# Attention and feed-forward on one core: from an order spread over loops and rates to one order made by a list scheduler in the kernel, with the first tiles transposed by TensorE

## The chip, the cores and the metric

The kernel runs on one NeuronCore of a Trainium2 chip. The time is device microseconds of one execution, from three runs; the trace is of one profiled execution. TensorE (PE) multiplies and takes a weight load before each matmul; VectorE (DVE), ScalarE (ACT) and GpSimd (POOL) do the element-wise work; SyncE (SP) issues the DMAs. Each engine works through its own instructions in the order in which they were written for it.

## The reference

Four batches, eight heads, 768 positions, head size 64. Attention is banded: a position sees the `n_global` = 8 first positions and the `n_local` = 96 positions up to itself, with a bias of a slope per head times the distance. The output, as 3,072 tokens of 512 values, goes through a layer norm and a feed-forward net of 512 to 2,048 to 512 with a residual.

```python
def _attn_ref(q, k, v, n_global, n_local):
    scores = scale * np.matmul(q, k.transpose(0, 1, 3, 2))
    keep = is_global | is_local
    scores = np.where(keep, scores + bias[None], -1e9)
    a = np.exp(scores - np.max(scores, axis=-1, keepdims=True))
    a = a / (np.sum(a, axis=-1, keepdims=True) + 1e-09)
    return np.matmul(a, v)

def _moe_ref(x, g_ln, w_ch1, w_ch2):
    xn = (x - mu) / np.sqrt(var + 1e-06) * g_ln
    return x + np.maximum(xn @ w_ch1, 0.0) @ w_ch2
```

The two weight matrices arrive as 64-bit floats, 16.8 MB together.

## The kernel before

A **tile** is 128 positions of one batch, all heads; there are 24, in the order of `TILES`: first tile 0 of batches 3, 2, 1, 0 (t = 0 to 3, the *first tiles*, which see one block of keys), then tiles 1 to 5 of each batch (t = 4 to 23), which see two blocks. A **chunk** c is two tiles, 256 tokens.

Every operand of a matmul is split into two fp16 parts, high and low, and three products of the four (four in the scores) are added up in PSUM.

**Attention of a tile** (`attention`): load k, q, v (256 KB each, L108); split them (ACT makes the high part, DVE or POOL the low one: L177/L178, L199/L200, L186/L187); transpose k and q by DMA (`kT`, `qT`, L180, L202) and copy q's halves by two DMAs (L208); then by groups of heads, two groups in a first tile and four in another: score matmuls (L234), mask and row minimum on DVE (L239), exponential on ACT (L243), split into `pn` (high part on ACT for t < 4, else on DVE, L246/L248; low part on POOL, L249), transpose by DMA (`pT`, L251), product with v (L259 to L261). Then the quotient (L265), and in `norm` the mean and variance (L272, L273), the power on POOL (L276), the scaling (L279 to L281) and a last DMA transpose into `xT` (L282).

**Feed-forward.** `ffn1` multiplies `xT` by w1 and puts a 512-column bank into two fp16 parts (L335 on ACT, L336 on DVE); `ffn2` multiplies by w2 (L344) and adds the residual (L348); L350 stores. For t < 4 `ffn1` goes tile by tile with 128 columns (the groups called `f` at L330 to L332), after that by chunk with 256 columns (`f_None`).

**Weights** (`weight`): 16 pieces of 1 MB, each loaded (L115) and put together by ACT, DVE, ACT, DVE, ACT, DVE (L151 to L157), in three buffers.

**What sets the order.** The loops write the work as generators. `run(main, side, rate)` takes `rate` steps of the side work for each step of the main work (0.6, 2.0, 2.0, 0.5 at the start, `RATE` = 1.6 after), one tile ahead (`AHEAD`); a dictionary `ORDER` ties single instructions to others. From that the framework's own scheduler (`schedule_with_timeline_sim=True`) makes the order of each engine. At the start this is

```python
    run(f1w(), tokens(1), 0.6)      # w1 pieces and ffn1 of tile 0, beside tile 1
    run(f1(1), tokens(2), 2.0)
    run(f1(2), tokens(3), 2.0)
    run(f2w(), f1(3), 0.5)          # w2 pieces, beside ffn1 of tile 3
    run(seq(ffn2(0, 1), ffn2(2), ffn2(3)), side(3 * CT + AHEAD), RATE)
    for c in range(2, NC):          # ffn(c): ffn1 of the chunk, ffn2 of its two tiles
        g = side((c + 2) * CT + AHEAD)
        run(ffn(c), extremes(g) if c == 3 else g, RATE)
```

All DMAs are issued from SP, in one queue.

Of the kernel before, what the change touches and what calls it, by code (L numbers as in the profile page):

```python
# [12 lines left out]
I32 = mybir.dt.int32  # L13
# [60 lines left out]

@with_exitstack
def banded(ctx, tc, q, k, v, n_global, n_local, g_ln, w1, w2, out, flag):
    nc = tc.nc
    vec, act, pool, sp, pe = nc.vector, nc.scalar, nc.gpsimd, nc.sync, nc.tensor
    load = sp
# [11 lines left out]
    def chain(prev, ins):  # L91
        if prev is not None:
            tc.add_manual_dep(ins.ins, prev.ins.name, NOSYNC, reason="groups of one bank in turn")
        return ins

    marks = {}

    def mk(key, ins):

        marks[key] = ins  # L100
        if ORDER.get(key) in marks:
            tc.add_manual_dep(ins.ins, marks[ORDER[key]].ins.name, NOSYNC, reason="order")

    place = {bi: t for t, bi in enumerate(TILES)}

    def fetch(src, name, b, i):
        f = p2.tile([P, H, D], F32, tag="ld", name=f"{name}f{b}_{i}", bufs=6)
        mk(f"L{place[b, i]}", load.dma_start(out=f, in_=src[b, :, i * P:(i + 1) * P, :].rearrange("h p d -> p h d")))  # L108
        return f

    early = {name: fetch(src, name, *TILES[0]) for name, src in (("k", k), ("q", q))}

    def piece(src, name):
        st = p3.tile([P, 2, 512], I64, tag="st", name="st" + name, bufs=3)
        mk("D" + name, load.dma_start(out=st, in_=src))  # L115
        return st

    def piece1(j, c):
        return piece(w1[2 * c * P:2 * (c + 1) * P, j * 512:(j + 1) * 512].rearrange("(a p) n -> p a n", a=2), f"1_{j}_{c}")

    early["w"] = piece1(0, 0)
    cnt = counts(tc, const, load, n_global, n_local)
    ng, nl = cnt[:, 0:1], cnt[:, 1:2]
# [15 lines left out]
    big = const.tile([P, NF], F32, name="big")  # L139
    less = const.tile([P, 1], F32, name="less")  # L140
    pool.memset(less, -0.5001)
    wm = const.tile([P, 16], F32, name="wm")

    def weight(st, dh, dl, name, n):

        words = st.rearrange("p a n -> p (a n)").bitcast(I32).rearrange("p (n two) -> p n two", two=2)
        lo, hi = words[:, :, 0], words[:, :, 1]  # L150
        mk("A" + name, act.activation(out=lo, in_=st.rearrange("p a n -> p (a n)").bitcast(U32).rearrange("p (n two) -> p n two", two=2)[:, :, 0], func=AF.Relu, scale=2.0 ** -29, bias=less))  # L151
        vec.scalar_tensor_tensor(out=lo, in0=hi, scalar=SIGN, in1=lo, op0=ALU.bitwise_and, op1=ALU.bitwise_or)
        act.activation(out=hi.bitcast(F32), in_=hi.bitcast(F32), func=AF.Abs, scale=2.0 ** -111, accum_out=big[:, n:n + 1])
        vec.scalar_tensor_tensor(out=hi, in0=hi, scalar=3, in1=lo, op0=ALU.logical_shift_left, op1=ALU.bitwise_or)
        u = st.bitcast(F32).rearrange("p a (n two) -> p a n two", two=2)[:, :, :, 1]
        act.activation(out=dh, in_=u, func=AF.Copy)
        vec.tensor_tensor(out=dl, in0=u, in1=dh, op=ALU.subtract)  # L157

    def weights1(j, c):
        sl, cs = slice(j * 512, (j + 1) * 512), slice(2 * c, 2 * c + 2)  # L160
        weight(piece1(j, c) if j or c else early["w"], w1h[:, cs, sl], w1l[:, cs, sl], f"1_{j}_{c}", 2 * j + c)

    def weights2(f):
        fs = slice(2 * f, 2 * f + 2)
        weight(piece(w2[2 * f * P:2 * (f + 1) * P, :].rearrange("(a p) n -> p a n", a=2), f"2_{f}"), w2h[:, fs, :], w2l[:, fs, :], f"2_{f}", NF // 2 + f)


    mv = const.tile([P, B * NT, 2], F32, name="mv")
    blocks = {}
# [12 lines left out]

    def values(b, i):
        vf = fetch(v, "v", b, i)
        vn = p2.tile([P, H, P], F16, tag="vn" if i else "vn0", name=f"vn{b}_{i}", bufs=3 if i else 2)
        act.activation(out=vn[:, :, :D], in_=vf, func=AF.Copy, scale=VS)  # L186
        vec.scalar_tensor_tensor(out=vn[:, :, D:], in0=vf, scalar=VS, in1=vn[:, :, :D], op0=ALU.mult, op1=ALU.subtract)  # L187
        return vn

    def attention(t, x, xT, at):  # L190
        b, i = TILES[t]
        if i == 1 and b:
            blocks[b, 0] = keys(b, 0), values(b, 0)
            yield
        kT = keys(b, i)
        qf = early["q"] if t == 0 else fetch(q, "q", b, i)
        yield
        qn = p2.tile([P, H, P], F16, tag="ld", name=f"qn{t}", bufs=6)
        act.activation(out=qn[:, :, :D], in_=qf, func=AF.Copy, scale=-QS)  # L199
        vec.scalar_tensor_tensor(out=qn[:, :, D:], in0=qf, scalar=-QS, in1=qn[:, :, :D], op0=ALU.mult, op1=ALU.subtract)  # L200
        qT = p2.tile([P, 2 * H, P], F16, name="qT")
        mk(f"q{t}", sp.dma_start_transpose(out=qT[:, :H, :], in_=qn.rearrange("p h d -> p (h d)")))  # L202
        yield
        for here, there in ((slice(0, D), slice(D, P)), (slice(D, P), slice(0, D))):
            if t == 0:
                vec.tensor_copy(out=qT[here, H:, :], in_=qT[there, :H, :])
            else:
                load.dma_start(out=qT[here, H:, :], in_=qT[there, :H, :])  # L208
# [12 lines left out]
        nm = p2.tile([P, H], F32, name="nm")
        mn = p2.tile([P, H], F32, name="mn")
        sm = p2.tile([P, H], F32, name="sm")
        r = p2.tile([P, H], F32, name="r")
        for g in range(H // gh):
            yield
            T = p2.tile([P, gh, W], F32, tag="T", name=f"T{t}_{g}", bufs=3)
            ps = ps_s.tile([P, gh, W], F32, tag="s", name=f"s{t}_{g}")
            last = None
            for u in range(gh):  # L230
                h = g * gh + u
                for n_ in range(nb):
# [441 lines left out]
```

## Time and profile before

| | |
|---|---|
| time, median of 3 runs | 698.7 us (697.59 to 702.15) |
| span of the profiled execution | 697.8 us |
| PE, DVE, ACT, POOL busy | 596.8, 392.7, 291.9, 157.5 us |
| mean granted clock of TensorE | 0.971 of full speed |
| DMA moved | 93.30 MB, 134 GB/s over the span |

The span runs from the first to the last instruction; the profiled execution's own time is not given beside it. Of the three runs the median is 0.9 us above the span. A busy PE is not PE at its peak: matmuls overlap, and the busy time is the union of their durations. "Idle before" is the time an engine stood still before an instruction, with what released it. A row's `f_None<-xT,w1h` means that a matmul writes `f_None` from `xT` and `w1h`.

### The profile page before, as it was taken

To read this page: it belongs to the slowest core of one execution; us is meant where nothing else is said; L and a number is where in the kernel's file an instruction comes from. 1 tells how busy PE (TensorE), PEld (TensorE's weight loads), DVE (VectorE), ACT (ScalarE), POOL (GpSimd) and SP (SyncE) were. 2 spreads that over 40 slices of the span, in tenths; PEclk is the share of its full clock that TensorE was granted. 3 is DMA by queue.
4 is the path that set the end of the run, shared out by engine and by line. 5 is a ranking of instruction groups with operands and counts; after the bars stand their busy time and mean duration, and the time that the engine had idled before them with its cause. 6 is when DMAs were issued, how large, how long until landed. Compare 5 with 4: busy or idle time off the path is not lost. (4 is left out here: it accounts for less than half of the span.)

```text
span 697.8 us, 14209 instructions
## 1 busy us (share of the span) xinstructions
PE 596.8 (86%) x5602; PEld 426.6 (61%) x5602; DVE 392.7 (56%) x976; ACT 291.9 (42%) x752; POOL 157.5 (23%) x141
## 2 busy tenths in 40 slices
PE   0107698998499988999999999899989999999995
PEld 0106576775377576587496586496576586694762
DVE  4887978725567777565456456365445456342111
ACT  4886959323424442354254254253243254140110
POOL 0111304213213313332221331222231232120000
PEclk9999799999599999999999999999999999999999
DMA  9999999936888766676948746856853855231001
GB/s 230 221 278 262 237 260 187 172 58 115 163 161 143 129 139 136 134 148 117 178 90 151 140 96 134 150 106 123 159 118 73 151 82 94 69 62 31 16 1 36
DMA packets 264731, 93.30 MB, mean 134 GB/s; under 512 B 254416, under 2 KB 254416, under 8 KB 264656
## 3 DMA queue, kind: packets, MB, share of 16 engines
q1 hardware_dynamic: 264656, 92.31, 65.2%
q8 instruction: 46, 0.75, 0.5%
q14 instruction: 29, 0.24, 0.1%
HBM read 37.23 MB, written 6.29 MB: 62 GB/s over the span
## 5 line engine op out<-in xcount | busy, mean ns | idle before, releaser
L344 PE MATMUL f<-w2h,h_None 128*128 128x512 f16 x640 | 197.0, 380 | 0.0
L330 PE MATMUL f_None<-xT,w1h 128*128 128x256 f16 x640 | 176.1, 275 | 2.9 <-DVE h_None L336 2.4
L331 PE MATMUL f_None<-xT,w1h 128*128 128x256 f16 x640 | 176.1, 275 | 0.0
L332 PE MATMUL f_None<-xT,w1l 128*128 128x256 f16 x640 | 175.9, 275 | 0.0
L249 POOL TENSOR_TENSOR pn<-T,pn 128x512 f16<-128x512 f32 x88 | 109.2, 1243 | 218.2 <-DVE pn L248 111.6
L344 PEld LDWEIGHTS <-h_None 128*128 128x128 f16 x960 | 91.9, 98 | 99.7 <-issue 1.6
L344 PE MATMUL f<-w2l,h_None 128*128 128x512 f16 x320 | 121.8, 381 | 0.0
L331 PEld LDWEIGHTS <-w1h 128*128 128x128 f16 x896 | 90.7, 101 | 28.6 <-issue 19.0
L330 PEld LDWEIGHTS <-w1h 128*128 128x128 f16 x896 | 90.8, 101 | 16.5 <-DMA xT<-xn 6.9
L332 PEld LDWEIGHTS <-w1l 128*128 128x128 f16 x896 | 90.8, 101 | 7.6
L243 ACT ACTIVATE T<-T,mn 128x256 f32<-128x256 f32 (+1 forms) x192 | 92.4, 484 | 3.6
L335 ACT ACTIVATE h_None<-f_None 128x512 f16<-128x512 f32 x80 | 47.2, 592 | 107.1 <-PE f_None L332 107.0
L336 DVE SCALAR_TENSOR_TENSOR h_None<-f_None,h_None 128x512 f16<-128x512 f32 x80 | 54.7, 684 | 50.8 <-ACT h_None L335 50.8
L239 DVE CUSTOM_DVE_ANT_0 T<-s,mask 128x256 f32<-128x256 f32 (+1 forms) x192 | 67.1, 396 | 25.5 <-PE s L234 25.0
L234 PE MATMUL s<-kT,qT 128*128 128x128 f16 x704 | 55.2, 226 | 25.5 <-DMA qT<-qn 14.2
L259 PE MATMUL pv<-vn,pT 128*128 128x64 f16 x352 | 40.9, 196 | 39.9 <-DMA pT<-pn 39.8
L234 PEld LDWEIGHTS <-qT 128*128 128x128 f16 x704 | 47.4, 101 | 34.6 <-DMA qT<-qn 14.3
L330 PE MATMUL f<-xT,w1h 128*128 128x128 f16 x256 | 50.4, 237 | 17.1 <-DMA xT<-xn 17.1
L248 DVE CAST pn<-T 128x512 f16<-128x512 f32 x80 | 39.9, 502 | 42.8 <-ACT T L243 39.0
L259 PEld LDWEIGHTS <-pT 128*128 128x128 f16 x352 | 32.4, 99 | 50.1 <-DMA pT<-pn 47.9
L178 POOL TENSOR_TENSOR kn<-kf,kn 128x512 f16<-128x512 f32 x20 | 25.5, 1273 | 121.0 <-ACT kn L177 121.0
L276 POOL TENSOR_TENSOR rs<-rs,half 128x1 f32<-128x1 f32 x24 | 22.4, 931 | 133.5 <-DVE rs L275 133.5
(96 smaller groups left out, 804.0 us busy)
## 6 DMA issues: line engine op xcount, KB each, us to landing
st<-in_moe_w_ch_dram SPq DMA_DIRECT2D x16, 1024.0 KB, 7.4
vf<-in_v_dram SPq DMA_DIRECT2D x27, 256.0 KB, 3.6
kf<-in_k_dram SPq DMA_DIRECT2D x26, 256.0 KB, 3.8
qf<-in_q_dram SPq DMA_DIRECT2D x24, 256.0 KB, 3.3
out_dram<-x SPq DMA_DIRECT2D x24, 256.0 KB, 2.4
qT<-qT SPq DMA_DIRECT2D x46, 128.0 KB, 2.4
pT<-pn SPq DMA_TRANSPOSE x88, 3.3
kT<-kn SPq DMA_TRANSPOSE x27, 4.1
```

Source lines behind the costliest of these rows:

```text
L234: last = chain(last, pe.matmul(ps[:, u, n_ * P:(n_ + 1) * P], lhsT=qT[:, a * H + h, :], rhs=use[n_][0][:, h, :], start=(a == 0), stop=(a = ...
L239: vec.tensor_tensor_reduce(out=T[:, u, :], in0=ps[:, u], in1=mask, scale=1.0 / Z, scalar=3e38, op0=ALU.add, op1=ALU.min, accum_out=nm[:, h ...
L243: mk(f"e{t}_{g}", act.activation(out=T[:, u, :], in_=T[:, u, :], func=AF.Exp, scale=-1.0, bias=mn[:, h:h + 1], accum_out=sm[:, h:h + 1]))
L248: vec.tensor_copy(out=pn[:, :, 0, :], in_=T)
L249: pool.tensor_tensor(out=pn[:, :, 1, :], in0=T, in1=pn[:, :, 0, :], op=ALU.subtract)
L259: last = chain(last, pe.matmul(pv[:, h, :], lhsT=ph, rhs=vv[:, h, :D], start=(n_ == 0), stop=False))
L330: last = chain(last, pe.matmul(ps[:, a], lhsT=w1h[:, kk, fs], rhs=xT[:, kk, cols], start=(kk == 0), stop=False))
L331: last = chain(last, pe.matmul(ps[:, a], lhsT=w1h[:, kk, fs], rhs=xT[:, NK + kk, cols], start=False, stop=False))
L332: last = chain(last, pe.matmul(ps[:, a], lhsT=w1l[:, kk, fs], rhs=xT[:, kk, cols], start=False, stop=(kk == NK - 1)))
L335: mk("h" + key, act.activation(out=hh[:, 0], in_=ps, func=AF.Relu))
L336: mk("l" + key, vec.scalar_tensor_tensor(out=hh[:, 1], in0=ps, scalar=0.0, in1=hh[:, 0], op0=ALU.max, op1=ALU.subtract))
L344: pe.matmul(ps, lhsT=hh[:, a, :], rhs=w, start=(f == 0 and n_ == 0), stop=(f == NF - 1 and n_ == 2))
```

## The change

Nothing is written in order any more. Each piece of work becomes an `Op` with its engine, an estimated duration, what it reads and writes, and a function that writes its instructions; a DMA also has an estimated transfer. `Plan.order` adds the edges that reused buffers bring, computes for each op the time that is still needed from its start to the end of the main chain (all ffn1 and ffn2 pieces, stretched by 1.13, plus 6 us for what feeds them), and then runs a list scheduler over PE, ACT, DVE, POOL and SP: on each engine, of the ops whose inputs are there, the one with the greatest need. Matmuls that read what a DMA brings are offered only 2 us after the estimated landing if something else is there. The ops are then written in that order inside `tc.manual_schedule()`, so that each engine keeps it.

```diff
-AHEAD = 1
-RATE = 1.6
+FEW = 2 * CT
-ORDER = {"D1_0_1": "q0", "L1": "q0", "L2": "p0_1", "L3": "p1_1"}
-ORDER.update({f"X{n}": f"l{2 + n // 8}_{2 * n % 16}" for n in range(16)})
+class Plan:
+    SEEN = {"DMA": 1.6, "PE": 0.25}
+    MARGIN = {"DMA": 2.0}
+    def order(self, chain, stretch, lead):
...
+        for o in reversed(line):
+            most = left.get(o, 0.0)
+            for p in o.behind:
+                extra = lead if p in rank and o not in rank else 0.0
+                most = max(most, need[p] + o.took + self.seen(o) + extra)
+            need[o] = max(most, o.took)
...
+        def offer(o):
+            t = max([o.after] + [end[p] for p in o.before])
+            m = max([t] + [end[p] + self.MARGIN["DMA"] for p in o.before if p.xfer is not None]) if o.engine == "PE" else t
+            known[o.engine].append((t, m, -need[o], place[o], o))
...
+                at = max(free[e], min(c[0] for c in known[e]))
+                now = [c for c in known[e] if c[1] <= at] or [c for c in known[e] if c[0] <= at]
+                c = min(now, key=lambda c: (c[2], c[3]))
...
+            free[e] = at + o.took
+            if o.xfer is not None:
+                dma = max(dma, free[e]) + o.xfer
+                end[o] = dma + self.SEEN["DMA"]
...
+    def split(ps, hi, lo, scale, r, w):
+        op("ACT", 0.64, lambda: act.activation(out=hi(), in_=ps(), func=AF.Copy, scale=scale), r=r, w=[(w, "hi")])
+        op("DVE", 0.72, low, r=[*r, (w, "hi")], w=[(w, "lo")])
+
+    def flip(src, r, name):
+        ps = psum(ps_2, "f2", [P, 4, P], name)
+        def emit():
+            for j in range(4):
+                pe.transpose(ps()[:, j, :], src()[:, j * P:(j + 1) * P], eye())
+        op("PE", 0.9, emit, r=[r, eye], w=[ps])
+        return ps
...
+    def first(ts):
...
+                f = raw[name, t]
+                ps = flip(lambda f=f: f().rearrange("p h d -> p (h d)"), f, f"{name}t{t}")
+                o = buf(p2, "kT0" if name == "k" else "qT", 2, [P, 2, 4, P], F16, f"{name}0_{t}")
+                split(ps, lambda o=o: o()[:, 0], lambda o=o: o()[:, 1], scale, [ps], o)
...
+                    for j in range(4):
+                        for n_, (a, c) in enumerate(((0, 0), (0, 1), (1, 0), (1, 1))):
+                            pe.matmul(ps()[:, j, :], lhsT=qT[side, a, j, :], rhs=kT[side, c, j, :], start=(n_ == 0), stop=(n_ == 3))
...
+                ps = flip(lambda T=T: T().rearrange("p j w -> p (j w)"), T, f"pt{t}_{e}")
+                pT = buf(p2, "pT", 4, [P, 2, 4, P], F16, f"pT{t}_{e}")
+                split(ps, lambda pT=pT: pT()[:, 0], lambda pT=pT: pT()[:, 1], 1.0, [ps], pT)
...
+                vec.tensor_scalar(out=xf(), in0=x().rearrange("p h d -> p (h d)"), scalar1=mv[:, t, 0:1], scalar2=rs(), op0=ALU.subtract, op1=ALU.mult)
+                vec.tensor_mul(out=xf(), in0=xf(), in1=gb)
...
+            ps = flip(xf, xf, f"xt{t}")
...
+    def ffn1(c, f):
+        n = CT * P
...
+    first(range(CT))
+    for j in range(NK):
+        for c_ in range(NK // 2):
+            weights1(j, c_)
+    first(range(CT, FEW))
+    for f in range(NF // 2):
+        weights2(f)
+    for c in range(2):
+        for f in range(0, NF, 2):
+            ffn1(c, f)
+    ffn2(0, 1)
+    ffn2(2, 3)
+    for t in range(FEW, B * NT):
+        attention(t)
+    for c in range(2, NC):
+        for f in range(0, NF, 2):
+            ffn1(c, f)
+        for n_ in range(CT):
+            ffn2(c * CT + n_)
...
+    line = plan.order(main, 1.13, LEAD)
+    with tc.manual_schedule():
+        for o in line:
+            o.emit()
+LEAD = 6.0
```

In the first tiles k, q, the exponentials and the normed x stay 32-bit floats, PE transposes them four 128 x 128 blocks at a time into a bank of `ps_2` (which ffn2 uses too), and ACT and DVE split them out of PSUM. Two heads lie in one block, so a score matmul there contracts 64 rows, and there are four products of the parts instead of a stacked pair. `ffn1` of tiles 0 to 3 is by chunk. Tile 4 loads and transposes k of batch 0's first tile again. `pT` has 4 buffers instead of 3; `mask0` and the identity `eye` lie in buffers of `h`. The low part of k of a reloaded first tile goes from DVE to POOL. The two counts are loaded from ACT's queue. The sixteen `extreme` reductions may not start before 250 + 10 n us of the plan.

## Rows read from the trace of the kernel before

**Rows 1.** The page: busy time of each engine with its share of the span and its instructions, and the span in 40 slices, PE's busy tenths.

```profile
span 697.8 us, 14209 instructions
...
PE 596.8 (86%) x5602; PEld 426.6 (61%) x5602; DVE 392.7 (56%) x976; ACT 291.9 (42%) x752; POOL 157.5 (23%) x141
...
PE   0107698998499988999999999899989999999995
```

**Rows 2.** The timeline of PE (start us, us, engine, line, operation, out<-in, shapes, count) in two dense stretches, and between them pieces of the chain that ended last (start us, us, what, count).

```profile
654.76 0.27 PE L330 MATMUL f_None<-xT,w1h 128*128 128x256 f16 x1
...
656.72 0.27 PE L330 MATMUL f_None<-xT,w1h 128*128 128x256 f16 x1
...
480.21 0.45 PE s L234 x8
...
627.77 20.72 PE f L344 x96
...
160.00 0.19 PE L259 MATMUL pv<-vn,pT 128*128 128x64 f16 x1
...
160.32 0.19 PE L261 MATMUL pv<-vn,pT 128*128 128x64 f16 x1
```

**Rows 3.** Instructions by tile or line: duration in ns (min/median/max), first and last start in us. The first two are ffn1 by chunk (t from 4 on) and by tile (t < 4), then the residual add.

```profile
L330 PE MATMUL f_None<-xT,w1h x640: 269/273/418, 189.4 to 673.5; 128*128 128x256 f16 x160
L330 PE MATMUL f<-xT,w1h x256: 216/219/314, 55.4 to 146.0; 128*128 128x128 f16 x128
...
L348 DVE SCALAR_TENSOR_TENSOR x<-f,x x24: 654/690/692, 135.7 to 690.2; 128x512 f32<-128x512 f32 x24
```

**Rows 4.** Windows: stretch in us, its length, busy us (instructions) of PE, PE's weight loads, DVE, ACT and POOL, granted clock, DMA's share, GB/s.

```profile
0.00:40.00 40.00, 5.76 (x56) 4.47 (x57) 26.18 (x67) 26.57 (x53) 4.33 (x11) 1.00 0.92 240
40.00:80.00 40.00, 18.16 (x238) 16.74 (x238) 35.85 (x73) 33.29 (x73) 5.73 (x4) 0.96 1.03 258
80.00:120.00 40.00, 34.60 (x389) 27.12 (x389) 33.09 (x53) 31.07 (x58) 12.49 (x8) 0.87 1.06 223
120.00:160.00 40.00, 39.23 (x459) 28.09 (x457) 21.67 (x48) 13.75 (x36) 10.08 (x8) 1.00 0.72 124
160.00:189.40 29.40, 17.55 (x184) 11.69 (x183) 18.25 (x56) 11.68 (x40) 7.76 (x7) 0.77 0.70 131
189.40:690.20 500.80, 481.35 (x4282) 338.51 (x4281) 256.56 (x678) 175.59 (x494) 117.10 (x104) 0.99 0.58 111
```

**Rows 5.** What PE waited for up to 189 us: us in total, times, longest us.

```profile
PE pv L259 <- DMA pT<-pn: 22.9, 9, 11.8
PE f L330 <- DMA xT<-xn: 17.1, 4, 15.5
PE s L234 <- DMA qT<-qn: 14.2, 2, 13.8
PE f L344 <- ACT w2h L156: 6.4, 2, 4.0
```

**Rows 6.** Groups of instructions by form over the whole span, costliest first: line, engine, operation, out<-in, shapes, count | busy us, mean ns of one | idle before us and what ended it. L152, L154 and L157 are the DVE steps of a weight piece, L336 and L335 split a bank of 512 columns out of PSUM.

```profile
L234 PE MATMUL s<-kT,qT 128*128 128x128 f16 x704 | 55.2, 226 | 25.5 <-DMA qT<-qn 14.2 <-DMA qT<-qT 4.1 <-DVE nm L239 4.1
L336 DVE SCALAR_TENSOR_TENSOR h_None<-f_None,h_None 128x512 f16<-128x512 f32 x80 | 54.7, 684 | 50.8 <-ACT h_None L335 50.8
...
L335 ACT ACTIVATE h_None<-f_None 128x512 f16<-128x512 f32 x80 | 47.2, 592 | 107.1 <-PE f_None L332 107.0
...
L152 DVE SCALAR_TENSOR_TENSOR st<-st 128x1024 int32<-128x1024 int32 x16 | 21.2, 1324 | 6.3 <-ACT st L151 6.2
L279 DVE SCALAR_TENSOR_TENSOR xs<-x,mv,gb 128x512 f32<-128x512 f32 x24 | 20.4, 849 | 0.0
...
L154 DVE SCALAR_TENSOR_TENSOR st<-st 128x1024 int32<-128x1024 int32 x16 | 19.6, 1222 | 1.6 <-ACT st L153 1.6
...
L157 DVE TENSOR_TENSOR w2l<-st,w2h 128x1024 f16<-128x1024 f32 x8 | 10.7, 1332 | 0.6 <-ACT w2h L156 0.6
L157 DVE TENSOR_TENSOR w1l<-st,w1h 128x1024 f16<-128x1024 f32 x8 | 9.7, 1213 | 2.4 <-ACT w1h L156 2.4
...
L178 DVE TENSOR_TENSOR kn<-kf,kn 128x512 f16<-128x512 f32 x7 | 4.8, 688 | 7.5 <-ACT kn L177 7.5
...
L206 DVE COPY qT<-qT 64x1024 f16<-64x1024 f16 x2 | 0.8, 422 | 0.0
```

**Rows 7.** One more window, and DVE's first instruction in the timeline.

```profile
40.00:60.00 20.00, 4.59 (x45) 4.59 (x45) 19.61 (x38) 17.91 (x38) 4.73 (x3) 1.00 0.97 249
...
4.81 0.69 DVE L178 TENSOR_TENSOR kn<-kf,kn 128x512 f16<-128x512 f32 x1 [4.81 <-ACT kn L177]
```

**Rows 8.** DMA: SP's issue of the transposes of pT and of the copies of qT (duration in ns, min/median/max, first and last start), and what the queue moved from 0 to 100 us (packets, MB, share of 16 engines).

```profile
L251 SPq DMA_TRANSPOSE pT<-pn x88: 1231/1264/2406, 26.5 to 623.0; - x88
...
L208 SPq DMA_DIRECT2D qT<-qT x46: 462/580/1467, 30.9 to 577.8; - x46
...
q1 hardware_dynamic: 39660, 24.34, 99.0%
```

**Rows 9.** What PE waited for from 189.4 us on, and the landing of pT after 200 us.

```profile
PE pv L259 <- DMA pT<-pn: 16.8, 19, 2.5
PE f_None L330 <- DVE h_None L336: 2.4, 2, 2.1
...
DMA to landing us min/median/max: 3.0/3.2/5.1
```

More of the change, by code (lines that the diff above doesn't have):

```diff
@@ L75, in banded @@
+LOOK = 0.5
+EAGER = 3.0
 @with_exitstack
@@ L89, in banded @@
     ps_2 = ctx.enter_context(tc.tile_pool(name="ps_2", bufs=2, space=PSUM))
[L91 to L108, printed above, removed]
-        return f
@@ L111, in banded @@
[L111 to L122, printed above, removed]
+    plan = Plan()
@@ new lines, in columns, with fetch, half_of @@
+    def columns(n, each):
+        return n * (each / 2400.0 + 0.0025)
+    def fetch(src, name, b, i, engine="SP"):
+        f = buf(p2, "ld", 6, [P, H, D], F32, f"{name}f{b}_{i}")
+        eng = act if engine == "ACT" else sp
+        dma(lambda: eng.dma_start(out=f(), in_=src[b, :, i * P:(i + 1) * P, :].rearrange("h p d -> p h d")), 1.6, w=[f], took=0.8, engine=engine)
+        return f
+    def half_of(t):
+        b, i = TILES[t]
+        return b, i
+    raw = {}
+    for name, src in (("k", k), ("q", q)):
+        raw[name, 0] = fetch(src, name, *TILES[0])
@@ L138, in banded @@
     w2l = const.tile([P, NF, DM], F16, name="w2l")
[L139 to L157, printed above, removed]
+    op("POOL", 0.8, lambda: make_identity(nc, eye()), w=[eye])
@@ L183, in values @@
[L183 to L187, printed above, removed]
-        return vn
-    def attention(t, x, xT, at):
+        weight(w2[2 * f * P:2 * (f + 1) * P, :].rearrange("(a p) n -> p a n", a=2), w2h[:, fs, :], w2l[:, fs, :], f"2_{f}", NF // 2 + f)
@@ L191, in attention, with join @@
+    def join(parts, whole):
+        plan.wrote[whole] = [o for p in parts for o in plan.wrote[p]]
+    xs, xTs, hs = {}, {}, {}
+    def attention(t):
         b, i = TILES[t]
-        if i == 1 and b:
-            blocks[b, 0] = keys(b, 0), values(b, 0)
-            yield
         kT = keys(b, i)
[L196 to L208, printed above, removed]
@@ L287, in tokens @@
+        op("DVE", 0.77, lambda: vec.scalar_tensor_tensor(out=xn()[:, 1, :], in0=xf(), scalar=rs(), in1=xn()[:, 0, :], op0=ALU.mult, op1=ALU.subtract), r=[xf, rs, (xn, "hi")], w=[(xn, "lo")])
         c, at = divmod(t, CT)
         if at == 0:
-            xTs[c] = p3.tile([P, 2 * NK, CT * P], F16, tag="xT", name=f"xT{c}", bufs=2)
-        xs[t] = xpool.tile([P, H, D], F32, tag="x", name=f"x{t}")
-        yield from attention(t, xs[t], xTs[c], at)
-    gs = const.tile([P, NK], F32, name="gs")
-    load.dma_start(out=gs, in_=g_ln.rearrange("(c p) -> p c", p=P))
@@ new lines, in banded @@
+    op("POOL", 0.1, lambda: pool.memset(ones, 1.0), w=["ones"], after=300.0)
+    op("DVE", 0.9, ranges, r=["cnt", *(("big", n_) for n_ in range(NF))], w=["ok"], after=450.0)
+    op("DVE", 1.0, products, r=["gs"], w=["wm", "wx"], after=460.0)
+    op("DVE", 0.7, limits, r=["wx"], w=["ok", "sums"], after=470.0)
+    op("DVE", 0.5, verdict, r=[("mv", t) for t in range(B * NT)], w=["ok", "sums"])
+    pf = psum(ps_1, "f1", [1, 3], "pf")
+    op("PE", 0.1, lambda: pe.matmul(pf(), lhsT=ones, rhs=sums, start=True, stop=True), r=["ones", "sums"], w=[pf])
```

657 lines of the change are left out of this document (417 added, 240 removed).

## The prediction

> **What bounds the kernel now.** I read the page first: PE is busy for 596.8 of 697.8 us, but the slices show that the first five and the eleventh are far from full [rows 1]. Busy time is a poor measure of pipelined matmuls, so I took the pitch, the distance from one start to the next, out of dense stretches [rows 2]: eighteen matmuls of 256 columns in 1.96 us are 0.109 us each; 96 of 512 columns in 20.72 us are 0.216; eight of 128 columns in 0.45 us are 0.056; eleven steps of 64 columns in 0.32 us are 0.029. The work by pitch: a chunk's ffn1 is 16 x 12 matmuls of 256 columns, 20.9 us; its ffn2 is 96 of 512 columns, 20.7; a tile that sees two blocks has 32 score matmuls and 48 products, 1.8 + 1.4 = 3.2 us.
>
> Then the marks in time [rows 3]: chunk 2's ffn1 begins at 189.4, the last residual add at 690.2. What PE still has to do from the first of these is ten chunks (416.4) and the attention of 18 tiles (57.3), **474 us**, in 500.8: only **27 us** are lost there. Ahead of it PE has ffn1 of four tiles in 128 columns (768 x 0.056 = 43), ffn2 of four tiles (41.5), attention of four first tiles (64 scores, 96 products: 6.4) and of two others (6.4): 97 us in 189.4, so **92 us are lost** before chunk 2. The windows [rows 4] say beside what: DVE is busy for 26.2 + 35.9 + 33.1 + 21.7 + 18.3 = 135.0 of 189.4 us (0.71) and ACT for 116.4, DMA is full to 120 us, PE is not. The waits name the releasers [rows 5]: until 189 us PE waits for transposing DMAs (pT 22.9 us, xT 17.1, qT 14.2), little for weights. So the first part is set by chains through DMA, ACT and DVE in which no engine is full, and behind it by DVE's sheer work; the second part is set by PE.
>
> **DVE's work before chunk 2.** It doesn't get less. Of it, 16 weight pieces cost 21.2 + 19.6 + 10.7 + 9.7 = 61.2 us [rows 6]. The split of pT out of PSUM is new for DVE (before, POOL made that low part): 8 x 0.684 by the row of a 512-column split out of PSUM = 5.5 us. The normed x of a first tile takes two instructions for one: four more, of nothing to 0.85 (the scaling with a scalar and a vector) each; I take 0.69, kn's subtraction, which it is nearest to by operands and size, so 2.8. Two copies for tile 0's qT go (0.8). The splits of k, q and x are the same count, from PSUM instead of SBUF (0.684 against 0.688: nothing). Sum 142.5 us. ACT's eight high parts of pn become eight of pT (0.59 each), so it stays at 116: not the bound.
>
> DVE starts at 4.8 us. With what fill? Before, 0.71 on the whole, 0.90 from 40 to 80 us, 0.98 at best [rows 4, 7]. With a scheduler that always has two chains (weights and tiles) to choose from, and shorter chains, I take the row of 0.90: chunk 2 at 4.8 + 142.5/0.90 = **163 us**; at 0.98 it is 150, at 0.71 it is 205. PE's own path allows it: ffn1 of chunk 0 now waits for tile 1 as well and begins when DVE has done two first tiles, masks and two pieces (about 32 us of work, so near 40 us, against 55.4); chunk 1 needs all four tiles and w1's eight pieces, about 77 us of DVE work or 90 us; behind it 20.9 + 41.5 + 6.4 us make 159.
>
> **What goes and what comes elsewhere.** Twenty DMA transposes (kT, qT, two pT and xT of four tiles) and six copies of qT leave SP's queue, 20 x 1.26 + 6 x 0.58 = 28.7 us of issuing [rows 8], and 5.2 + 0.8 MB (256 and 128 KB each) leave DMA; nearly all of it ran in the first 100 us, where 24.3 MB at 99% are on the queue [rows 8]. So the loads of weights and of tiles 4 and 5 come sooner; without it DVE would stay short of input. One load of k with its split and transpose comes in for tile 4, on SP behind the loads of that tile; POOL, busy for 10 of 80 us at the start [rows 4], gets its low part and loses eight of pn. Two small loads move from SP's to ACT's queue, ahead of ACT's first split, on which DVE waits until 4.8 us [rows 7]: two issues, at worst 1.2 us by the copies' row.
>
> PE gets 80 transposes of 32-bit blocks, which the trace doesn't show. Nearest is a 128-column matmul: 0.056 us at the pitch, 0.226 by itself [rows 2, 6], so 4.5 to 18 us; I take 18, since they come four at a time and are waited for. Sixty-four more score matmuls (contracting 64 rows) are 3.6 us, ffn1 of four tiles in 256 columns is 384 x 0.109 = 41.9 for 43. All of it lies ahead of chunk 2, where PE has 92 us to spare and would keep 163 - 118 = 45: nothing on the sum. Below nothing they don't go, as no PE work is taken out. Were that cover gone (PE bound from 40 us on), they would cost their 18 us.
>
> [...]
>
> **The steady part.** It has the same PE work, 474 us. Of the 27 us lost, 16.8 are waits for pT in 19 of the products, 2.4 for h, and the rest is mostly the clock (0.99 over 500.8 us) [rows 4, 9]. A pT lands 3.0 to 5.1 us after its issue [rows 9]; the new order puts the product at least 1.3 + 1.6 + 1.6 us behind its issue by the plan, and 2 us more if other work is there. So most of these waits should go: I take **10 us** (4 to 25). The sixteen `extreme` reductions and the tail's small DVE work lie in DVE's idle half (256.6 busy of 500.8 us); if it were full there, PE would wait for h.
>
> **Sum.** 163 + 474 + 10 + 7.6 from the start of the last residual add to the span's end (690.2 to 697.8, unchanged: the last add and store) + 0.9 by which the median stands above the span = **655 us**.
>
> **The rivals.**
> *Better fill.* DVE at 0.98 and 4 us lost: 150 + 474 + 4 + 8.5 = 636. For it: DVE did it for 20 us. Against: only there.
> *Half the fill.* In-order ACT and DVE hand each piece to and fro six times, three weight buffers allow no more than three pieces under way, and a fixed order can't take what happens to be ready: fill 0.80, chunk 2 at 183, 15 lost, 680. The same time would come of the clock: if the transposes leave it at half while ffn1 of both first chunks runs, its 41.9 us take 83.8, and PE's path is 40 + 83.8 + 41.5 + 6.4 + 10 for the transposes and scores of tiles 2 and 3, 182 us. Against it: 0.96 with a PE less than half busy [rows 4]. [...]
> *No gain at the start.* Fill stays 0.71, chunk 2 at 205: 698, no change. For it: the fill was low with a scheduler before too. Against: DMA, then full, is relieved of a fifth.
> *Slower.* The order is fixed from estimates, and PE meets each of the 80 later products (20 tiles x 4) before its pT has landed, with everything queued behind it on PE. Before it was 16.8/80 = 0.2 us each. From 0.75 us each, 60 us in place of my 10, the kernel is over 1% slower; at 0.9 it is 718. It decides only if DVE, ACT or SP run behind the plan all the time; they have idle halves, which speaks against it.
> *The order isn't kept*, and the framework sorts anew: then only the first tiles' shorter chains remain. I put them at a third of the 54 us that PE waited for qT, pT and xT [rows 5], 18 us: 680.
>
> **How the numbers follow.** Chances: forecast 0.55 (643 to 670), better fill 0.15, half the fill or the clock 0.13, no gain 0.07, slower 0.07, order not kept 0.03. The likeliest is 655. Leaving out some 0.1 on either side gives 636 to 687. One per cent, 7 us, is about what a measurement can tell here; faster by more than that are the forecast, better and half fill and the order not kept: 0.86; within it 0.07; slower 0.07.
>
> **What would show it.** First matmul of ffn1 near 40 us; chunk 2's (the first ffn1 that follows an xT made by DMA) near 163; DVE's busy share before it near 0.9; DMA below full in the first 100 us; waits of PE for pT after it under 5 us; transposes of 0.06 to 0.23 us. I'd be wrong if chunk 2 starts on time but the 474 us stretch by more than 25, or if DVE's share stays at 0.7.

## The result, and the profile after

The changed kernel takes **653.96 us** (median of 4 runs, 653.24 to 655.26) against 698.14 us of the kernel before beside it (695.75 to 702.15): ratio 0.9364, 95% interval 0.9326 to 0.9403. Forecast were 655.0 us and a range of 636 to 687.

First the page of after (busy us, share, instructions; PE's busy tenths in 40 slices; the DMA queue's packets, MB, share), to lay beside [rows 1].

```profile
span 653.5 us, 13626 instructions
...
PE 607.1 (93%) x5362; PEld 432.5 (66%) x5362; DVE 407.3 (62%) x983; ACT 290.8 (45%) x753; POOL 148.9 (23%) x139
...
PE   6478669979999999999999999999999999999995
...
q1 hardware_dynamic: 245904, 87.06, 64.6%
```

The hole that was at the eleventh slice is gone, and so are the eights that follow it. What is left lies in the first nine slices.

The marks, which answer to [rows 3]: ffn1 by line (ns min/median/max, first and last start in us), the PE timeline where chunk 2 begins (start us, us, line, out<-in), and the residual add.

```profile
L635 PE MATMUL f<-xT,w1h x768: 272/273/421, 38.8 to 624.3; 128*128 128x256 f16 x192
...
172.99 0.61 PE L590 MATMUL s<-kT,qT 128*128 128x128 f16 x8
173.44 0.27 PE L635 MATMUL f<-xT,w1h 128*128 128x256 f16 x1
...
L667 DVE SCALAR_TENSOR_TENSOR x<-f,x x24: 671/688/693, 145.9 to 645.6; 128x512 f32<-128x512 f32 x24
```

The first ffn1 is at 38.8 us (before 55.4). A chunk has 64 of L635's matmuls, so the 129th is chunk 2's first: 173.4 us (before 189.4). From there to the last ffn2's end are 472.1 us, and 8.0 more to the span's end: 173.4 + 472.1 + 8.0 = 653.5.

Windows, as [rows 4] (stretch, length, busy us of PE, weight loads, DVE, ACT, POOL, granted clock, DMA share, GB/s):

```profile
0.00:40.00 40.00, 21.46 (x157) 17.09 (x158) 27.81 (x85) 27.77 (x70) 3.39 (x12) 1.00 0.75 191
40.00:80.00 40.00, 30.54 (x249) 24.16 (x249) 34.45 (x70) 33.86 (x75) 2.93 (x2) 0.87 0.75 218
80.00:120.00 40.00, 34.29 (x328) 29.39 (x327) 34.58 (x57) 28.62 (x53) 3.77 (x4) 0.91 0.56 147
120.00:150.00 30.00, 25.15 (x174) 12.56 (x173) 28.80 (x49) 19.62 (x43) 10.01 (x8) 0.91 0.86 183
150.00:173.40 23.40, 23.40 (x177) 12.42 (x176) 12.51 (x31) 5.62 (x18) 5.03 (x5) 0.97 0.78 168
173.40:645.90 472.50, 472.25 (x4286) 336.89 (x4283) 268.37 (x691) 175.34 (x498) 123.77 (x109) 1.00 0.63 118
```

PE is full from 150 us on, before chunk 2 begins, and stays so to the end. All but some 0.7 us of what is lost is lost ahead of 150. What PE waited for in the whole span (us, times, longest), against [rows 5, 9]:

```profile
PE xt L401 <- DVE xs L527: 13.1, 3, 7.4
PE f L635 <- DVE h L643: 6.5, 1, 6.5
PE kt L401 <- DMA kf<-in_k_dram: 4.8, 2, 4.7
PE f L658 <- DVE x L667: 3.9, 1, 3.9
PE pt L401 <- DVE pT L388: 3.3, 1, 3.3
```

No wait for a pT that DMA brings is left (before 22.9 us up to 189 and 16.8 behind it). The pT of after land 3.1/3.4/5.5 us (min/median/max) after their issue from 174 us on, no sooner than before; the products come later. With issues and first products paired in their order, a product starts 6.5/11.7/22.7 us behind the issue of its pT, in before, from 200 us on, 3.1/4.1/6.1.

### The profile page after: what moved, and what is told of

Same layout as the page of the kernel before. It is cut to its first block, busy times and chain, and to the rows that moved or that the text cites. A ratio compares the mean times of both kernels' runs of the same rounds, so it can differ in the third digit from the quotient of the medians.

```text
span 653.5 us, 13626 instructions
## 1 busy us (share of the span) xinstructions
PE 607.1 (93%) x5362; PEld 432.5 (66%) x5362; DVE 407.3 (62%) x983; ACT 290.8 (45%) x753; POOL 148.9 (23%) x139
## 4 chain that ended last, share of the span: by engine, by line
PE 84%; DVE 6%; ACT 4%; DMA 3%; issue 1%; SPq 0%; POOL 0%; DVEq 0%
PE f L658 35%; PE f L637 12%; PE f L636 12%; PE f L635 12%; PE s L590 5%; PE pv L426 2%; PE pv L427 2%; PE pv L425 2%; DMA kf<-in_k_dram 1%; DMA st<-in_moe_w_ch_dram 1%; ACT T L462 1%; DVE w1l L369 1%; PE s L496 1%; DVE T L457 1%; ACT st L343 1%
## 5 line engine op out<-in xcount | busy, mean ns | idle before, releaser
L658 PE MATMUL f<-w2h,h 128*128 128x512 f16 x768 | 248.5, 382 | 3.9 <-DVE x L667 3.9
L635 PE MATMUL f<-xT,w1h 128*128 128x256 f16 x768 | 212.8, 277 | 7.7 <-DVE h L643 6.5
L636 PE MATMUL f<-xT,w1h 128*128 128x256 f16 x768 | 212.7, 277 | 1.7 <-DVE xT L544 1.7
L637 PE MATMUL f<-xT,w1l 128*128 128x256 f16 x768 | 212.7, 277 | 0.9 <-DVE w1l L369 0.9
L658 PEld LDWEIGHTS <-h 128*128 128x128 f16 x1152 | 108.2, 98 | 116.9 <-issue 8.5
L658 PE MATMUL f<-w2l,h 128*128 128x512 f16 x384 | 146.6, 382 | 1.0 <-DVE w2l L369 1.0
L596 POOL TENSOR_TENSOR pn<-T,pn 128x512 f16<-128x512 f32 x80 | 95.2, 1192 | 199.5 <-DVE pn L595 119.7
L643 DVE SCALAR_TENSOR_TENSOR h<-f,h 128x512 f16<-128x512 f32 x96 | 65.8, 686 | 99.5 <-ACT h L642 99.4
L642 ACT ACTIVATE h<-f 128x512 f16<-128x512 f32 x96 | 57.0, 594 | 140.4 <-PE f L637 140.3
L635 PEld LDWEIGHTS <-w1h 128*128 128x128 f16 x768 | 76.5, 100 | 19.6 <-ACT h L642 6.7
L636 PEld LDWEIGHTS <-w1h 128*128 128x128 f16 x768 | 76.4, 99 | 11.5
L449 POOL TENSOR_TENSOR rs<-rs,half 128x1 f32<-128x1 f32 x24 | 22.7, 946 | 156.8 <-DVE rs L446 156.8
L460 ACT ACTIVATE mn<-nm 128x2 f32<-128x2 f32 (+1 forms) x88 | 17.5, 199 | 79.3 <-DVE nm L457 79.3
L437 DVE TENSOR_TENSOR x<-pv,r 128x512 f32<-128x512 f32 x24 | 16.5, 689 | 46.9 <-PE pv L427 46.9
```

The source lines that it names most:

```text
L596: op("POOL", 1.25, lambda pn=pn, T=T: pool.tensor_tensor(out=pn()[:, :, 1, :], in0=T(), in1=pn()[:, :, 0, :], op=ALU.subtract), r=[T, (pn, ...
L635: pe.matmul(ps()[:, a], lhsT=w1h[:, kk, fs], rhs=xT()[:, kk, :], start=(kk == 0), stop=False)
L636: pe.matmul(ps()[:, a], lhsT=w1h[:, kk, fs], rhs=xT()[:, NK + kk, :], start=False, stop=False)
L637: pe.matmul(ps()[:, a], lhsT=w1l[:, kk, fs], rhs=xT()[:, kk, :], start=False, stop=(kk == NK - 1))
L642: op("ACT", 0.6, lambda: act.activation(out=hh()[:, 0], in_=ps(), func=AF.Relu), r=[ps], w=[(hh, "hi")])
L643: op("DVE", 0.7, lambda: vec.scalar_tensor_tensor(out=hh()[:, 1], in0=ps(), scalar=0.0, in1=hh()[:, 0], op0=ALU.max, op1=ALU.subtract), r= ...
```

## The experiments

To compare kernels I count PE's **lost** time up to 180 us: 180 less the matmuls begun by then, each at its pitch in [rows 2], a transpose at 0.11. A lost us is either idle time or a matmul at half pace: many matmuls take longer and stand further apart (256 columns in 421 ns and 0.213 us apart, not 273 and 0.109; over one such stretch of after, 59.45 to 62.85 us, the granted clock is 0.50). For those the pitch is counted once more under "half pace", an upper bound, as some stand alone. Times in us; chunk 1 and chunk 2 are the starts of their first ffn1 (for chunk 1 that of tile 2, where ffn1 goes tile by tile), "behind" goes from chunk 2 to the end of the last ffn2.

| kernel | median | ratio to before | first ffn1 | chunk 1 | chunk 2 | behind | lost to 180 | of it half pace |
|---|---|---|---|---|---|---|---|---|
| before | 698.1 | 1 | 55.4 | 113.7 | 189.4 | 500.8 | 82.2 | 10.1 |
| after | 654.0 | 0.936 | 38.8 | 94.3 | 173.4 | 472.1 | 62.4 | 19.9 |
| e1_list_only | 659.1 | 0.943 | 70.1 | 114.1 | 178.6 | 472.1 | 80.4 | 8.1 |
| e2_flip_only | 734.0 | 1.051 | 43.2 | 120.1 | 225.6 | 497.1 | 97.6 | 15.6 |
| e3_not_kept | 699.2 | 1.000 | 61.3 | 143.1 | 208.4 | 481.1 | 97.0 | 18.2 |
| e4_no_slack | 667.9 | 0.956 | 38.6 | 96.7 | 172.8 | 486.1 | 61.9 | 17.3 |
| e5_flip2 | 655.3 | 0.940 | 39.5 | 95.2 | 173.5 | 472.1 | 53.6 | 14.3 |
| e6_pool_w2 | 649.4 | 0.931 | 38.8 | 92.7 | 169.2 | 470.5 | 56.7 | 15.3 |
| e7_pool_w1 | 652.4 | 0.936 | 40.1 | 91.2 | 170.0 | 471.3 | 58.3 | 15.2 |
| e8_chain | 654.3 | 0.939 | 46.1 | 65.2 | 172.8 | 471.3 | 61.3 | 20.9 |
| e9_chain_w2 | 657.4 | 0.942 | 46.2 | 65.6 | 177.3 | 470.5 | 64.7 | 22.7 |
| e10_pool_both | 656.7 | 0.942 | 40.4 | 96.9 | 177.4 | 471.5 | 66.1 | 18.7 |
| e11_chain_both | 657.3 | 0.943 | 46.2 | 63.9 | 175.5 | 470.9 | 63.3 | 19.2 |
| e12_list_w2 | 659.6 | 0.945 | 69.4 | 114.7 | 182.1 | 471.3 | 82.9 | 10.9 |

**One part alone.** The list order with first tiles split in SBUF and transposed by DMA, as before the change:

```diff
-                ps = flip(lambda f=f: f().rearrange("p h d -> p (h d)"), f, f"{name}t{t}")
+                    dma(lambda o=o, n=n: sp.dma_start_transpose(out=o(), in_=n().rearrange("p h d -> p (h d)")), 1.6, r=[(n, "hi"), (n, "lo")], w=[o], took=1.3)
...
-                ps = flip(lambda T=T: T().rearrange("p j w -> p (j w)"), T, f"pt{t}_{e}")
+                dma(lambda pn=pn, pT=pT: sp.dma_start_transpose(out=pT(), in_=pn().rearrange("p j a w -> p (j a w)")), 1.6, r=[(pn, "hi"), (pn, "lo")], w=[pT], took=1.3)
```

> The list order alone: tiles 0 to 3 are split in SBUF and transposed by DMA again, as in the kernel before. Theory (the order carries most, by keeping products behind their transposes): PE loses under 5 us after chunk 2's first ffn1, which comes at 180 to 190 us; 660 to 670 us. Rival (the shorter chains of the first tiles carry the start): chunk 2 no earlier than the 189 us of before and DMA full in the first 100 us; 672 us or more.

And the old loops and the framework's scheduler, with first tiles by PE:

```diff
+        if t < 2 * CT:
+            yield from first(t, x, xT, at)
+            return
...
+            split(flip(f.rearrange("p h d -> p (h d)"), f"{n}t{t}"), o[:, 0], o[:, 1], scale)
```

> The transposes by PE alone: tiles 0 to 3 as in the changed kernel, loops, rates and the framework's scheduler as before. Theory: chunk 2 moves up by 5 to 12 us from 189, the 27 us lost after it stay: 685 to 695 us. Rival (first tiles carry the start): chunk 2 at 173 or earlier, 680 us or less. If the shorter chains gave nothing by themselves: 698.

Measured 659.1 (ratio 0.940 to 0.946) and 734.0 (1.048 to 1.054). **The list order carries nearly all of the gain; the transposes by PE add 5 us to it and, with the old order, cost 35**, which none of the three expectations had. With the list order go the fourth pT buffer and ffn1 by chunk for tiles 0 to 3; no run takes these apart. What PE waited for in the list-only kernel, and its first two windows:

```profile
PE s L506 <- DMA qT<-qn: 29.7, 2, 23.0
PE f L625 <- DMA xT<-xn: 16.7, 2, 14.1
PE s L506 <- DMA qT<-qT: 8.0, 2, 4.8
...
0.00:40.00 40.00, 2.77 (x22) 2.17 (x23) 23.76 (x57) 26.87 (x54) 3.53 (x12) 1.00 1.01 234
40.00:80.00 40.00, 16.41 (x147) 13.43 (x146) 33.61 (x68) 29.97 (x68) 10.61 (x8) 1.00 1.10 254
```

DMA is as full as before and ffn1 begins 31 us later than in after, yet chunk 2 only 5. The table says why: its PE is idle for 72 us (80.4 - 8.1) against 42 (62.4 - 19.9), 30 more, but it has 12 us fewer at half pace and some 12 less to do (80 transposes at 0.11 and 64 score matmuls at 0.056): 30 - 12 - 12 = 6.

In the flip-only kernel, PE's waits and the two windows ahead of its late chunk 2:

```profile
PE xt L198 <- DVE xs L263: 27.2, 3, 12.0
PE pv L339 <- DMA pT<-pn: 17.3, 23, 2.0
PE pt L198 <- ACT T L239: 15.1, 7, 10.9
...
160.00:200.00 40.00, 40.00 (x336) 23.25 (x334) 8.31 (x15) 2.52 (x4) 0.99 (x1) 1.00 0.18 34
200.00:225.60 25.60, 14.74 (x141) 10.50 (x139) 15.00 (x53) 11.86 (x43) 7.92 (x7) 0.68 0.65 130
```

A transpose on PE is a link of the first tile's chain: it waits for xs (27.2 us) or T (15.1), and ffn1 stands behind it on the same engine. The second cost is further on: from 160 to 200 us PE is full with feed-forward work while DVE is busy for 8.3 us and DMA for 0.18, so little of the attention of tiles 4 and 5 is being prepared, and from 200 us on PE stands idle for 11 of 25.6 us before chunk 2 begins. All of the loss lies ahead of chunk 2: it is 36 us later than in before, and the time behind it is what it was.

**The order given but not kept.** All ops written in the list's order, but outside the block that keeps it:

```diff
-    with tc.manual_schedule():
-        for o in line:
-            o.emit()
+    for o in line:
+        o.emit()
```

> The same pieces written in the list's order, but the framework's scheduler sorts them anew. Theory (the kept order is what removes PE's waits): waits for pT come back, 15 to 27 us lost after chunk 2: 668 to 685 us. Rival (written order and dependencies are enough): 652 to 657 us.

Measured 699.2: no change from before (0.998 to 1.002). PE's waits in it, the last line from chunk 2 (208.4 us) on:

```profile
PE xt L401 <- DVE xs L527: 22.9, 3, 17.6
PE xt L401 <- DVE rs L446: 13.2, 1, 13.2
...
PE pv L425 <- DMA pT<-pn: 0.6, 1, 0.6
```

The same instructions wait 36.1 us for xs and rs instead of 13.1. Keeping the order is worth 45 us, 35 of them ahead of chunk 2 and 9 behind it. The expectation had it otherwise: the waits for pT didn't come back (0.6 us), and the part behind chunk 2 is 20 us shorter than in before (481.1 for 500.8), though nothing keeps the list's order. What shortens it there, no run tells.

**No slack for DMA.** The planner takes a transfer as landed when it is over, and adds no margin ahead of PE:

```diff
-    SEEN = {"DMA": 1.6, "PE": 0.25}
-    MARGIN = {"DMA": 2.0}
+    SEEN = {"DMA": 0.0, "PE": 0.25}
+    MARGIN = {"DMA": 0.0}
```

> The plan's allowance after a DMA is taken away: landing 0.0 instead of 1.6 us after the transfer, margin for PE 0.0 instead of 2.0. Theory (this allowance keeps each product behind its transpose): PE waits for pT again, 5 to 20 us in all: 659 to 675 us. Rival (a product that isn't urgent comes late anyway, since PE is full): within 3 us of 654.

Measured 667.9 (0.953 to 0.958), 14 us more. Chunk 2 comes as early as in after, at 172.8; all 14 are behind it (486.1 for 472.1). PE's waits:

```profile
PE xt L401 <- DVE xs L527: 11.9, 3, 6.3
PE pv L425 <- DMA pT<-pn: 9.5, 6, 2.3
PE f L635 <- DVE h L643: 9.0, 2, 7.4
```

The waits for pT are back, 9.5 us in 6; another 3.3 were counted as half pace behind such gaps. So the kept order has no gaps in its second part only with this slack. Of the 29 us by which that part is shorter than in before it accounts for 14: without it the part still is 15 us shorter than in before (486.1 for 500.8).

**Each transpose twice:**

```diff
-            for j in range(4):
-                pe.transpose(ps()[:, j, :], src()[:, j * P:(j + 1) * P], eye())
+            for j in range(8):
+                pe.transpose(ps()[:, j % 4, :], src()[:, j % 4 * P:(j % 4 + 1) * P], eye())
```

> Every transpose by PE is made twice: 80 more, some 9 us of PE at the changed kernel's trace. Theory (PE has 62 us to spare before 150 us): 0 to 2 us more. Rival (they lie in the chains that set chunk 2): 4 to 9 us more.

Measured 655.3 (0.937 to 0.943): 1.3 us more for 80 more transposes, within what a measurement tells here. Their cost is covered, as forecast, but in part by another thing: less half pace, 14.3 us for 19.9. The last section shows the rows.

**Less work for DVE.** The low parts of w2's eight pieces on POOL, then those of w1's eight:

```diff
-ON_POOL = ()
+ON_POOL = tuple(f"2_{f}" for f in range(8))
```

```diff
-ON_POOL = ()
+ON_POOL = tuple(f"1_{j}_{c}" for j in range(4) for c in range(2))
```

> The low part of w2's eight pieces is made on POOL: DVE has 8 x 1.22 = 9.8 us less before chunk 2, between 90 and 136 us. Theory of the prediction (DVE's work sets chunk 2): chunk 2 some 10 us earlier, 642 to 647 us. Rival (PE's path from the first 100 us sets it; PE lost only 7 us after 100): at most 7 us less, rather 0 to 4: 650 to 656 us.

> The low part of w1's eight pieces is made on POOL: DVE has 9.8 us less up to 75 us, each piece's chain is longer by some 2 us. Theory (DVE's work sets chunk 2): 642 to 647 us. Rival (PE's path from the first 100 us sets it, through tiles 2 and 3): also 6 to 10 us less, with chunk 1 at 85 to 88 instead of 94.3 us; so this run and the one with w2 tell the two apart together. If the longer chain of a piece counts more: 655 to 660.

**An earlier chunk 1.** ffn1 of chunks 0 and 1 interleaved by column group of w1:

```diff
-    for c in range(2):
-        for f in range(0, NF, 2):
-            ffn1(c, f)
+    for j in range(NK):
+        for c in range(2):
+            for f in (4 * j, 4 * j + 2):
+                ffn1(c, f)
```

> Only the order of the main chain for the first two chunks: ffn1 by groups of 512 columns of w1, each group for both chunks, so that tiles 2 and 3 are needed at once. If PE's path sets the start: chunk 1 begins before 75 us, PE is full from there and chunk 2 comes 5 to 15 us earlier: 640 to 650 us. If DVE's work sets it, it only changes its order: 652 to 657 us.

Measured 649.4 (0.929 to 0.934), 652.4 (0.933 to 0.938) and 654.3 (0.937 to 0.941). Eight low parts less on DVE were meant to take 9.8 us of work from it; they gave 4.6 us and 1.5, the second within what a measurement tells. A chunk 1 that begins 29 us earlier (65.2 for 94.3) gave nothing: from 100 us on PE waits there for pieces of w2 (4.5 us), a pT (5.1) and a residual add (3.0), in after for 1.0, 0 and 3.9. After these I held that DVE's work and PE's own path kept chunk 2 about equally late. If so, taking both away must give more than either; the combinations of the edits above:

> ffn1 of chunks 0 and 1 interleaved by column group, and the low parts of w2 on POOL. If chunk 2 is held by two things about equally late, PE's own path (chunk 1's ffn1 at 94.3 us) and DVE's work, each edit alone is stopped by the other and both together gain more than their sum (0 and 4.6): chunk 2 near 164, 644 us. If it is DVE's work alone, the interleaving adds nothing: 649. If interleaving only moves PE's loss to the wait for w2, and POOL (2.15 us for 1.3) makes w2 later still: 652 to 655.

> All 16 low parts of the weights on POOL: DVE has 20 us less before chunk 2, POOL 34 us more. If DVE's sheer work held chunk 2: 20/0.89 = 22 us earlier than 173.4, but no earlier than PE's path (159 by the prediction, 164 by chunk 1's start of about 91): 643 to 645. If the gains of the two halves (4.6 and 1.5) were the same few us: 649. If they simply add: 648.

> The interleaving and all 16 low parts on POOL. If DVE's work and PE's path hold chunk 2 together, this is the best of all: chunk 2 near 160, 640 us. If chains between ACT, DVE and POOL set the pace of the weight pieces (three buffers, six steps), taking work from DVE no longer helps: 648 to 650.

> The list order with first tiles transposed by DMA (659.1 us) and the low parts of w2 on POOL. If that kernel is held by DMA and the landings of the first tiles' transposes in its first 114 us, its end of the part before chunk 2 still has w2's pieces to do, and it gains as the changed kernel did: 654 to 655. If its chunk 2 is held by the loads alone (DMA full to 80 us): 659.

Measured 657.4 (0.938 to 0.947), 656.7 (0.937 to 0.946), 657.3 (0.938 to 0.947) and 659.6 (0.940 to 0.950). **The forecast of that theory failed**: with all 16 low parts on POOL the kernel is 7 us slower than with w2's alone, with both edits it is no better, and the list order without transposes by PE gains nothing from w2's on POOL (659.6 for 659.1). But these runs took little from DVE. Up to chunk 2 it is busy for 138.1 us in after, for 135.0 and 137.0 with eight low parts on POOL, for 134.4 with all 16, and for 138.0 and 133.1 with the interleaving and eight or 16: 5 us less at most, where 10 and 20 were meant. In the kernel with all 16 there, 17 of DVE's instructions ahead of chunk 2 are over a quarter and 0.15 us longer than their median, each beside one of POOL, such as the second L527 here (start us, us, instruction):

```profile
34.06 0.69 DVE L527 TENSOR_TENSOR xs<-xs,gb 128x512 f32<-128x512 f32 x1
...
34.82 2.37 POOL L367 TENSOR_TENSOR w1l<-st,w1h 128x1024 f16<-128x1024 f32 x1 [0.76 <-ACT w1h L365]
...
35.24 2.50 DVE L527 TENSOR_TENSOR xs<-xs,gb 128x512 f32<-128x512 f32 x1
```

By an estimate from the median of each instruction over the kernels, DVE's instructions ahead of chunk 2 are 9 us too long in after and 19 us in this kernel, and its new order puts 4 us of later tiles' work ahead of chunk 2. So whether less work for DVE would bring chunk 2 sooner, these runs don't tell. PE's waits in the kernel with all low parts on POOL:

```profile
PE xt L401 <- DVE xs L527: 14.2, 4, 5.2
PE f L635 <- DVE h L643: 5.9, 2, 3.3
PE kt L401 <- DMA kf<-in_k_dram: 5.2, 2, 5.0
PE pt L401 <- DVE pT L388: 3.9, 1, 3.9
PE pv L425 <- DVE vn L575: 3.3, 1, 3.3
```

They are much like those of after: the chains of the first tiles (k in, pT, xs) and waits for a bank put into h; new is a wait for a later tile's vn, which the new order puts late. DVE is not out of these waits. In after's three longest behind the first load (7.43 us for xs, 6.47 for h, 4.31 for xs) it is busy for 7.26, 6.35 and 4.14 us, and ahead of the xs at 35.05 three of its steps belong to weight pieces:

```profile
27.63 1.22 DVE L355 SCALAR_TENSOR_TENSOR st<-st 128x1024 int32<-128x1024 int32 x1
...
29.36 1.22 DVE L347 SCALAR_TENSOR_TENSOR st<-st 128x1024 int32<-128x1024 int32 x1
...
32.51 1.21 DVE L369 TENSOR_TENSOR w1l<-st,w1h 128x1024 f16<-128x1024 f32 x1
```

In the table idle time (lost less half pace) is 40 to 47 us in after and in all six of these kernels that transpose by PE, whatever was meant to come off DVE; the 57 to 66 that they lose in all differ through half pace (15 to 23 us) and through where the planner's new order leaves a wait. A version that beats both kernels is there, the eight low parts of w2 on POOL at 649.4, against 655.3 and 654.3 of two kernels that stand level with after and ran beside it; from 120 to 150 us it has lost the waits of after for w2l (1.0 us) and for a residual add (3.9), and at 168.8 us it has one of 2.6 for nm. How much of that is relief of DVE and how much a lucky order isn't shown.

## Why the prediction was right, step by step

**The time.** 655.0 was forecast, 654.0 measured, but the sum holds two errors of 10 us that cancel: chunk 2 at 173.4 where it says 163, and nothing lost behind it where it says 10. That the total came within 1 us is luck. Its other terms fit: 474 us of PE work against 472.1, and 7.6 + 0.9 at the end against 8.0 + 0.5 (median less span).

**First marks, right.** ffn1 at 38.8 (forecast 40), chunk 1 at 94.3 (90).

**Chunk 2, 10 us late.** The step that failed is "behind it by DVE's sheer work", priced as 142.5 us at a fill of 0.90. The work was right: DVE was busy for 27.81 + 34.45 + 34.58 + 28.80 + 12.51 = 138.2 us by 173.4. The fill was not: 138.2 of the 168.6 us from 4.8 on are 0.82, nearer to the 0.80 of the rival *half the fill* than to 0.90. By windows it was 0.70, 0.86, 0.86, 0.96 and 0.53: the row of 0.90 was taken from the middle of the old kernel's first part, and held for the middle of the new one, but not for its ends. Nor is DVE's sum all of the bound: over the last 23.4 us PE is full and DVE half idle. Chunk 2 comes when PE has done its own 111 us of work and lost 62, some 42 idle and up to 20 at half pace. Of the waits, 38.6 us in all, 25 are in the first tiles' chains (loads of k and q, pT, vn, xs, xT), 6.5 for a bank of h, 3.9 for a residual add and 3 for weight pieces. DVE works through the longest of them, as shown above, so its order and its work ahead of xs and h can be what makes PE wait; the runs with low parts on POOL don't decide it, as they hardly relieved DVE. None took a step from the chain of x, its moments and xs, on which PE waits longest, so where the 42 could be shortened stays open.

**Half pace, not priced.** The sum puts PE's work ahead of chunk 2 at full pitch, and weighs the clock only for ffn1 of both chunks, as a rival at 680. That transposes might leave the clock at half was supposed, not shown: before has no transpose on PE, and its trace shows only that the granted clock can be half, 0.50 from 80.4 to 87.1 us. ffn1 of chunk 0 did start at half pace (256 columns 0.213 us apart), but left it at 45.6 us; with the transposes and scores ahead of it and the stretches behind later gaps the price was up to 20 us. It didn't vanish in PE's 45 spare us, since a PE that is full from 150 us on gets nothing back. The forecast's argument against the clock, 0.96 with a PE less than half busy, rested on a column that reads 1.00 ahead of the first clock record of before and of after, over matmuls at half pace too (last section). In before that record begins at 59.9 us: from 55.5 us to there the column reads 1.00 and a matmul of 128 columns takes 311 ns, behind it 216; from 60 to 80 us, where records are, it reads 0.91.

**The steady part, a mis-sized term.** The forecast said that most of the pT waits should go, and kept 10 us (4 to 25). All went. The plan's slack has a part in it, as argued: without it 14 us come back (e4), near the middle of that range. It isn't the only way, since e3, whose order isn't the plan's, has 0.6 us of these waits.

**Transposes, right in size.** The groups of L401 by form are busy for 17.7 us in all, for 80; I took 18, from bounds of 4.5 to 18, and hidden. Doubling them cost 1.3 us.

**The DMA relief, wrong in consequence.** From 0 to 100 us the queue moves 18.55 MB at 71.0%, as the forecast had it below full against 24.34 MB at 99% [rows 8]. But "without it DVE would stay short of input" counts for little: with DMA full to 80 us (e1) DVE is busy for 23.8 instead of 27.8 us in the first 40, and the list order loses 5 us in all.

**Rivals.** *The order isn't kept* was put at 680, with 18 us for shorter chains alone. It gives 699.2: with the order not kept those chains gain nothing, and under the old loops they cost 35 us (734.0). The forecast took a transpose on PE as shorter for everyone; it missed that PE works in order (in after it starts all its 5,361 matmuls and transposes in the order in which they were written), so that whatever waits for a first tile's T or xs (15.1 and 27.2 us in e2) now holds ffn1 too. *Slower*, by late pT, did not come: 0 us of such waits in 80 products. *No gain at the start* and *better fill* did not come either; of *half the fill* the fill itself came, and half pace in part, but chunk 2 at 173.4, not at 183.

## What to carry to other kernels

Ask of a path's end which engine is full just ahead of it, and count what that engine loses, by the waits that end last. A helper engine's sum and fill over a whole stage don't tell when it makes another wait: here DVE was busy for 0.82 of the stage, and for 17.75 of the 18.2 us of PE's three longest waits behind the first load. When work is moved to another engine, read what the first one gained before concluding from the time: 20 us meant were 4 to 5 here. The list order was worth its gain only where it was kept (45 us), and without slack for what lands late it lost 14 us. A step moved from DMA to PE shortened a chain here (the first ffn1 at 38.8 us, not 70.1) but also let that chain block what was queued behind it; it paid (5 us) with an order that allowed for it, and cost 35 without.

## What the runs showed of the hardware

**Half pace ahead of the first clock record.** The PE timeline of after at the first transposes, and in the ffn1 of chunk 0:

```profile
4.67 1.09 PE L401 MATMUL kt<-eye,kf 128*128 128x128 f32 x4 [4.67 <-DMA kf<-in_k_dram]
6.63 1.12 PE L401 MATMUL qt<-eye,qf 128*128 128x128 f32 x4 [0.88 <-DMA qf<-in_q_dram]
...
45.37 0.42 PE L636 MATMUL f<-xT,w1h 128*128 128x256 f16 x1
45.58 0.37 PE L637 MATMUL f<-xT,w1l 128*128 128x256 f16 x1
45.79 0.27 PE L635 MATMUL f<-xT,w1h 128*128 128x256 f16 x1
45.90 0.27 PE L636 MATMUL f<-xT,w1h 128*128 128x256 f16 x1
```

Until 45.6 us the starts of these matmuls of 256 columns are 0.21 us apart, then 0.11. The view prints a granted clock of 1.00 for that stretch (40 to 44 us), but no clock was recorded in it: the trace's first clock record begins at 45.78 us, where the pitch changes. In before it begins at 59.9, again where the half pace first ends. Later the column does show such stretches, as in these windows of after around chunk 1's start and behind the wait at 146.7 us:

```profile
90.00:97.00 7.00, 5.61 (x36) 4.56 (x35) 6.13 (x8) 2.91 (x4) 0.53 (x1) 0.51 0.43 89
146.00:152.00 6.00, 5.33 (x14) 1.97 (x14) 5.97 (x13) 2.69 (x9) 3.44 (x4) 0.53 1.00 230
```

So in these two traces the half pace ahead of the first record is read from the pitch, not from the column.

**The pitch behind transposes.** In the kernel that does each twice, PE ran nothing but 32-bit transposes from 4.67 to 8.65 us:

```profile
4.67 1.94 PE L401 MATMUL kt<-eye,kf 128*128 128x128 f32 x8 [4.67 <-DMA kf<-in_k_dram]
6.68 1.97 PE L401 MATMUL qt<-eye,qf 128*128 128x128 f32 x8
8.44 1.18 PE L401 MATMUL kt<-eye,kf 128*128 128x128 f32 x8
...
10.06 0.95 PE L496 MATMUL s<-k,q 64*128 64x128 f16 x14 [0.22 <-DVE q L390]
```

Two groups of eight take 1.94 and 1.97 us, the third 1.18, and fourteen scores behind it 0.95 (0.056 apart; in after 0.107 at that place). In this trace the full pace came in the third group, with nothing on PE before it but 32-bit transposes; in after, where the first groups of four stand 0.88 and 0.18 us apart, it had not come by the scores at 8.95 us. In after a transpose starts 0.213 us behind the one before it at half pace (the groups up to 38.6 us) and 0.109 at full pace (those at 48.4 and 54.1 us).
